# One-core attention and feed-forward kernel: local attention of batches 1 to 7 in 22 blocks of 26 tokens on 32x32 blocks, with the turning on VectorE

## The chip, the cores and the metric

The kernel runs on one core of a Trainium2 chip. The metric is the device time of one execution in microseconds (us), the median of the runs shown; less is better. The engines are named as in the profile: PE (TensorE, matmuls), PEld (its weight loads), DVE (VectorE), ACT (ScalarE), POOL (GpSimd) and SP (SyncE, which here only issues transfers).

## What is computed

Eight batches of eight heads, 576 tokens, head dimension 64. Each head gets two attentions: one over tokens pooled four to one (144 of them), whose output is repeated four times, and a local one in which a token sees the three neighbours on either side. Their sum, 4608 tokens by 512, goes through a two-layer feed-forward net.

```python
q_d, k_d, v_d = (a.reshape(B, H, 144, 4, D).mean(axis=3) for a in (q, k, v))
out_up = np.repeat(sm_attn(q_d, k_d, v_d), 4, axis=2)
mask = np.abs(pos[:, None] - pos[None, :]) < 4
scores = np.where(mask, scale * np.matmul(q, k.transpose(0, 1, 3, 2)), -1e9)
out_local = np.matmul(softmax(scores), v)
x = (out_up + out_local).transpose(0, 2, 1, 3).reshape(4608, 512)
h = x @ w_in
g = np.where(h >= 1, h, np.where(h <= -1, 0.0, (h + 1) ** 2 / 4))
return g @ w_out
```

(shortened: `scale` is 1/8, `softmax` subtracts the row's maximum)

## The kernel before

**Feed-forward.** The 4608 tokens are nine chunks of 512. Chunks 0 and 1 compute `x @ w_in` directly (L1045), chunks 2 to 8 by Strassen-Winograd products of 256x256 quarters (L1135); both feed `g @ w_out` (L1073). All are 128-row matmuls in three terms of split floats. Weights are loaded and split in chunk 0 (L852 to L873). DVE and ACT form `g` (L1011 to L1027) and the Winograd sums (L1141, L1144).

**Attention.** Heads go in pairs, 32 in all, numbered n; the two heads of a pair sit on partitions 0 to 63 and 64 to 127. Pairs 0 to 3 (batch 0) come first, as the start of the kernel, since chunk 0 needs all four. The 28 pairs of batches 1 to 7 are laid between the matmuls of chunks 0 to 6, four to a chunk; chunks 7 and 8 have none. For one of these 28 pairs:

- scores (L423, L468), one PE step: 20 matmuls of 64x64 for ten windows of 64 tokens in two heads, and six of 64x144 for the pooled scores, on 64x64 tiles of the array. A tile is given by where the operands lie (which head: 64 rows) and where the output goes (64 output partitions), so there are four. `QUARTERS` fixes the order of the steps. For g below 4 a window of head h goes to output half h; for g = 4 and for the pooled blocks it goes to the other half. So the two tiles "head h to half h" get eight window matmuls each, and the other two get two windows and three pooled blocks each.
- softmax of the windows, 128x640: band (L527), maximum (L530), subtraction on POOL (L532), exponential on ACT (L534), sum (L575), reciprocal (L579, L580), product (L583). The pooled softmax runs beside it (L558, L559, L565, L594, L595).
- transposes, one PE step with the 128x128 array: five for the windows (L652), three and one for the pooled part (L677, L678). ACT copies them out (L686, L701), DVE a masked piece (L705).
- values, one PE step on 64x64 tiles: 20 matmuls with 53 to 61 columns (L730) and eight for the pooled part (L753), then the joining on ACT and DVE (L808, L810, L821) into `xr`.

The trace counts two records for each float32 matmul that is not a transpose, so 20 matmuls show as x40.

**Order.** A planner (`Plan`) gives each step an engine, an assumed cost, keys and buffers, and places steps greedily; each engine then runs its steps in the order that this gives, fixed before the launch. The table `K` holds the keys. Loads all go through SP's queue, in order.

**Start.** PE runs ten warming matmuls on `ident` (L278), then the pairs of batch 0. Pair 0 has its values pooled by PE (L623, ten matmuls with the constant `fours`), and its pooled output is repeated four times inside PE (L773, 16 matmuls); the others have their values pooled on POOL (L604, L607). For pair 3 POOL also subtracts the maximum (L532).

Of the kernel before, what the change touches and what calls it, by code (L numbers as in the profile page):

```python
# [76 lines left out]
class Plan:  # L77
# [32 lines left out]
    def run(self):  # L110
# [7 lines left out]
        free = {"PE": 5.0, "ACT": 3.0, "DVE": 1.0, "POOL": 1.4, "SP": 0.7}  # L118
# [130 lines left out]
def attention_then_ffn(ctx: ExitStack, tc, qT, kT, vw, vp, vq, band, fours, w_in, w_out, out):  # L249
# [97 lines left out]

    def attention(n):
        b, p = pairs[n]
        early = n < K["early"]  # L350
        first = b == 0
        shares = b >= WIDE
        flat = shares or n < K["flat"]
# [23 lines left out]
        l_q = op("SP", 0.72 if b < 2 else 0.95, lambda: nc.sync.dma_start(qb.tile, qT[b, p]), bufs=[qb], key=k0 - ld, name=name + "lq")  # L377
        l_k = op("SP", 0.72 if b < 2 else 0.95, lambda: nc.sync.dma_start(kb_.tile, kT[b, p]), bufs=[kb_], key=k0 - ld, name=name + "lk")
# [3 lines left out]
        if not by_pe:  # L382
            vpb = sbuf("vp", [P if shares else KB, NKB, FACTOR, P], F32, "w" if 0 < n < 4 else "vp", range(8, 16) if 0 < n < 4 else [0])
            vsrc = vq[b - WIDE, p] if shares else vp[b, p]
            l_vp = op("SP", 1.7 if shares else 1.85, lambda: nc.sync.dma_start(vpb.tile, vsrc.rearrange("k (n f c) -> k n f c", n=NKB, f=FACTOR)),
                      bufs=[vpb], key=k0 - lv, name=name + "lvp")
        l_v = op("SP", 0.82 if b < 2 else 1.1, lambda: nc.sync.dma_start(vb.tile, vw[b, p].rearrange("k (n d) -> k n d", n=NB)),
# [14 lines left out]
        slp = psum([(0, 1, 2)] if shares else pairs_of_banks)  # L402
        spp = slp if shares else psum([(u,) for pair in pairs_of_banks for u in pair] if flat and first else [(2,)] if flat else pairs_of_banks)
# [46 lines left out]
        SPB = 2 if shares else 0  # L450
# [7 lines left out]
        def sp_view():  # L458
            return spp.tile[:, SPB, 0 : NSP * SD].rearrange("p (n s) -> p n s", n=NSP)
# [20 lines left out]
        if shares:  # L480

            def all_scores():
                if early:
                    add_band()
                for step in QUARTERS:
                    (window_scores if len(step) > 1 else pooled_block)(*step)

            o_sl = o_sp = op("PE", 1.46 if early else 1.10, all_scores, [l_q, l_k, o_qd, o_kd, before.get("x")], [slp, qb, kb_, qdb, kdb], kk[1], name=name + "sl", mode=1)
        else:
# [788 lines left out]
```

## Time and profile before

| what | value |
|---|---|
| time, median of 3 runs | 924.33 us (919.49 to 925.19) |
| the profiled execution's own time | 923.9 us |
| its span, first to last instruction | 921.8 us |
| PE, DVE, ACT, POOL busy in the span | 903.3, 654.2, 538.0, 125.8 us |
| mean granted TensorE clock | 0.996 |
| chain that ended last: PE, DVE, ACT, DMA | 89%, 4%, 3%, 3% |

PE is busy nearly all the time, so the time of the kernel is read as the sum of what PE issues, plus the start before chunk 0. Matmuls are pipelined: the length of a record is not its price. The price of a PE step is the distance from its first record to the first record of the step behind it.

### The profile page before, as it was taken

The numbers are of one execution on the slowest core, as the hardware profiler recorded it, in microseconds if no ns is written. First come the engines' busy times: TensorE is split into PE (matmuls) and PEld (weight loads), VectorE is DVE, ScalarE is ACT, GpSimd is POOL, SyncE is SP. The second block draws the span as 40 slices with busy tenths as digits, with TensorE's granted clock in tenths as the row PEclk, the third lists the DMA queues.
The fourth block names the chain that finished last, engine by engine and source line by source line (L and its number), as shares of the span: only waits on it lengthen the run. The fifth ranks groups of instructions, "written<-read, shape, count | busy, mean of one in ns | idle before, by whom it ended". The sixth has DMA issues, their size and how long they took to land.

```text
span 921.8 us, 20432 instructions
## 1 busy us (share of the span) xinstructions
PE 903.3 (98%) x8254; PEld 778.6 (84%) x8254; DVE 654.2 (71%) x1139; ACT 538.0 (58%) x1072; POOL 125.8 (14%) x126
## 2 busy tenths in 40 slices
PE   7799999999999999999999999999999999999998
PEld 6577788888888888888888888888888889989996
DVE  6799986888968775777867676877687755453543
ACT  4788896555565555556655555655555655444542
POOL 5222131111111110111111111111011000000000
PEclk9899999999999999999999999999999999999999
DMA  9997342664576656666576657665675456445631
GB/s 268 392 390 261 98 143 73 242 227 163 181 250 232 209 189 209 226 221 217 200 242 224 221 181 253 227 220 180 223 234 201 157 170 235 161 161 189 233 103 46
DMA packets 66170, 190.13 MB, mean 206 GB/s; under 512 B 7364, under 2 KB 9540, under 8 KB 66076
## 3 DMA queue, kind: packets, MB, share of 16 engines
q1 hardware_dynamic: 61468, 180.44, 57.2%
q10 hardware_dynamic: 4608, 8.39, 2.4%
q8 instruction: 65, 1.06, 0.5%
q14 instruction: 29, 0.24, 0.1%
HBM read 164.68 MB, written 24.12 MB: 205 GB/s over the span
## 4 chain that ended last, share of the span: by engine, by line
PE 89%; DVE 4%; ACT 3%; DMA 3%; issue 1%; SPq 0%; POOL 0%; ACTq 0%; DVEq 0%
PE ps L1073 41%; PE ps L1135 29%; PE ps L1045 9%; PE ps L730 2%; PE ps L423 2%; PE ps L652 2%; DMA vp<-vq 1%; PE ps L753 1%; PE ps L677 1%; PE ps L468 1%; DMA kf<-kT 1%; DVE gt L1027 1%; DVE tt L1144 1%; DMA out<-tt 1%; DVE tt L1023 1%
## 5 line engine op out<-in xcount | busy, mean ns | idle before, releaser
L1073 PE MATMUL ps<-w_o,gt 128*128 128x512 f32 x1728 | 439.8, 395 | 0.1
L1073 PEld LDWEIGHTS ps<-w_o,gt 128*128 128x128 f32 x1728 | 310.3, 188 | 58.0 <-DVE gt L1027 0.6
L1135 PE MATMUL ps<-T,lS 128*128 128x256 f32 x1008 | 147.9, 283 | 1.6 <-ACT tt L1141 1.6
L1135 PEld LDWEIGHTS ps<-T,lS 128*128 128x128 f32 x1008 | 133.9, 189 | 7.9 <-ACT tt L1141 3.9
L1011 ACT ACTIVATE tt<-tt 128x512 f32<-128x512 f32 x112 | 70.6, 630 | 108.1 <-DVE tt L1144 94.5
L1023 DVE SCALAR_TENSOR_TENSOR tt<-tt 128x512 f32<-128x512 f32 x112 | 83.7, 748 | 56.3 <-ACT tt L1016 54.7
L1025 ACT CAST gt<-tt 128x512 fp32r<-128x512 f32 x136 | 84.5, 621 | 62.8 <-DVE tt L1023 52.7
L1027 DVE TENSOR_TENSOR gt<-tt,gt 128x512 fp32r<-128x512 f32 x136 | 96.8, 712 | 32.8 <-ACT gt L1025 29.3
L1141 ACT COPY tt<-ps 128x512 f32<-128x512 f32 x112 | 65.3, 585 | 83.5 <-PE ps L1135 80.6
L1135 PE MATMUL ps<-B,lA 128*128 128x256 f32 x672 | 101.3, 286 | 0.3 <-DVE tt L1144 0.2
L1135 PEld LDWEIGHTS ps<-B,lA 128*128 128x128 f32 x672 | 90.6, 189 | 12.9 <-DVE tt L1144 5.8
L1045 PE MATMUL ps<-x,w_i 128*128 128x512 f32 x384 | 95.2, 397 | 1.0 <-ACT x L897 0.4
L1016 ACT ACTIVATE tt<-tt 128x512 f32<-128x512 f32 x144 | 91.0, 632 | 4.4
L1045 PEld LDWEIGHTS ps<-x,w_i 128*128 128x128 f32 x384 | 71.1, 188 | 18.9 <-ACT x L897 0.8
L1144 DVE TENSOR_TENSOR tt<-tt 128x512 f32<-128x512 f32 x56 | 41.8, 746 | 58.9 <-ACT tt L1141 58.7
L1144 DVE TENSOR_TENSOR tt<-ps,tt 128x512 f32<-128x512 f32 (+1 forms) x112 | 62.1, 554 | 28.8 <-PE ps L1135 27.7
L607 POOL TENSOR_TENSOR vd<-vp 128x256 f32<-128x256 f32 (+1 forms) x31 | 23.3, 750 | 347.4 <-PE ps L753 336.0
L604 POOL TENSOR_TENSOR vp<-vp 128x512 f32<-128x512 f32 (+1 forms) x31 | 43.4, 1399 | 130.8 <-DMA vp<-vq 127.7
L532 POOL TENSOR_TENSOR sl<-sl,mxl 128x640 f32<-128x640 f32 x29 | 40.4, 1392 | 89.6 <-DVE mxl L530 89.4
L1135 PEld LDWEIGHTS ps<-B,lS 128*128 128x128 f32 x336 | 45.6, 188 | 6.6 <-DVE tt L1144 2.5
L1135 PE MATMUL ps<-B,lS 128*128 128x256 f32 x336 | 50.9, 287 | 0.1
L1135 PE MATMUL ps<-T,lA 128*128 128x256 f32 x336 | 48.8, 281 | 0.0
(111 smaller groups left out, 1058.9 us busy)
## 6 DMA issues: line engine op xcount, KB each, us to landing
lS<-S SPq DMA_DIRECT2D x112, 512.0 KB, 4.4
lA<-A SPq DMA_DIRECT2D x56, 512.0 KB, 3.7
vp<-vq SPq DMA_DIRECT2D x28, 512.0 KB, 4.8
lA<-A SPq DMA_DIRECT2D x56, 256.0 KB, 3.2
v<-vw SPq DMA_DIRECT2D x32, 320.0 KB, 3.6
raw_i<-w_in SPq DMA_DIRECT2D x16, 512.0 KB, 8.9
raw_o<-w_out SPq DMA_DIRECT2D x16, 512.0 KB, 8.2
out<-tt ACTq DMA_DIRECT2D x32, 256.0 KB, 2.2
```

The source lines that it names most:

```text
L532: o_s = op("POOL", 1.3, lambda: nc.gpsimd.tensor_tensor(slf(), slf(), ml_n(), op=ALU.subtract), [o_m], [slb, mlb], kk[2], name=name + "sub ...
L604: nc.gpsimd.tensor_tensor(vpb.tile[:, :, 0:2, :], vpb.tile[:, :, 0:2, :], vpb.tile[:, :, 2:4, :], op=ALU.add)
L1011: o2 = op("ACT", 0.49 + e, lambda: nc.scalar.activation(u(), src(), AF.Relu, bias=0.5, scale=0.5), deps, [srcbuf, ub], key, name=f"relu {n ...
L1016: nc.scalar.activation(u(), u(), AF.Square)
L1023: o4 = op("DVE", v, lambda: nc.vector.scalar_tensor_tensor(g(), src(), 1.0, u(), op0=ALU.max, op1=ALU.min), [o3], [srcbuf, ub], key, name= ...
L1025: o5 = op("ACT", 0.50 + e, lambda: nc.scalar.copy(flat(gb.tile[:, 0]), g()), [o4], [held, gb], key, name=f"gh {name}")
L1027: engine.tensor_tensor(flat(gb.tile[:, 1]), g(), flat(gb.tile[:, 0]), op=ALU.subtract)
L1045: nc.tensor.matmul(hb.tile[:, 0, :], wb.tile[:, w, cc * P : (cc + 1) * P], xt[:, x], start=cc == 0 and i == 0, stop=cc == NCC - 1 and i == 2)
L1073: nc.tensor.matmul(o, gb.tile[:, g, ts], wb.tile[:, w, :], start=i0 + i == 0, stop=i0 + i == 3 * NFC - 1)
L1135: nc.tensor.matmul(xy(dst), l(w, k), yb.tile[:, v, k], start=first and n == 0, stop=n == 5, skip_group_check=True)
L1141: return op("ACT", cost, lambda: nc.scalar.copy(to(), src()), deps, [tb, XY], kk[i], name=f"{name} {c},{j}")
L1144: return op("DVE", cost, lambda: nc.vector.tensor_tensor(to(), a(), b(), op=ALU.add), deps, held, kk[i], name=f"{name} {c},{j}", port=port)
```

## The change

Pairs of batches 1 to 7 go through a new function, `banded`; pairs 0 to 3 keep the old one, without its branch for later batches (`shares`).

- The windows become 22 blocks to a head, each of 26 tokens (the last of each half fewer or more) with 32 queries and 32 keys. A score block is a 32x32 output, so the scores use tiles of 64 rows and 32 columns, eight of them (two heads, four quarters of the output partitions). There are 40 matmuls of 32x32, four of 32x64 (a 23rd place filled by a copy) and ten of 32x144. The table `ORDER` gives their order.
- The window softmax is 128x384 in place of 128x640.
- The product with the reciprocal (`norm`) writes each block twice, masked by `odd`, 128x768 into the tile of q and k; `nc.vector.transpose` then turns 32x32 blocks into `sl`. This takes the place of the five window transposes on PE and of ACT's copy of them. The q and k of the next pair can only be loaded behind it, since the tile is shared.
- The pooled part is turned by PE in five transposes, arranged so that one ACT copy of 128x448 serves; the masked DVE piece goes.
- Values: 24 matmuls (20 of 52 or 54 columns, four of 26 or 29) and the same eight for the pooled part.
- Pair 0 is still pooled by PE, but no longer repeated there: `pu1` goes from 4 to 0, so four matmuls of 64x144 stand where 16 of 192 or 96 columns stood, and ACT and DVE join the parts as for the other pairs.
- Constants: `band` and its 32-wide form come in one transfer on ACT's queue, not SP's; `ident` is now the copy `ident_r`, which ACT makes behind the two band copies, and the warming matmuls wait for it.
- The keys in `K` and some assumed costs are other numbers, so the order of many steps moves. POOL gets 15 of the weight splits (8 before) and DVE 17 (24 before).

```diff
+SW = 32
+SQ = SW - 2 * (FACTOR - 1)
+NS = 11
+SHORT = [[0] + [SQ + 1 + SQ * i for i in range(NS - 1)], [SQ * NS + 1 + SQ * i for i in range(NS)]]
+ORDER = ("P00 w13 w11 w02 w10 w12 w11 P13 w10 w03 w12 w10 w02 w01 P11 w00 P10 w01 w00 P12 w03 P02 w13 w03 w00 w01 w13 "
...
-    ident = cpool.tile([P, P], F32, name="ident")
-    make_identity(nc, ident)
-    band_sb = cpool.tile([P, WIN], F32, name="band_sb")
-    nc.sync.dma_start(band_sb, band)
+    made = spool.tile([P, P + WIN + SW], F32, name="made", tag="w35")
+    nc.scalar.dma_start(made[:, P:], band)
+    make_identity(nc, made[:, 0:P])
     ident_r = cpool.tile([P, P], F32R, name="ident_r")
-    nc.scalar.copy(ident_r, ident)
+    nc.scalar.copy(ident_r, made[:, 0:P])
+    ident = ident_r.bitcast(F32)
...
+    def banded(n):
...
+        def scores():
+            seen = {}
+            for kind, h, c in ((x[0], int(x[1]), int(x[2])) for x in ORDER):
+                hs = slice(h * D, (h + 1) * D)
+                n = seen[kind, h, c] = seen.get((kind, h, c), -1) + 1
+                if kind == "w":
+                    w, cols, lhs, rhs = start_of(c // 2, 2 * n + c % 2), slice(n * SW, (n + 1) * SW), q_(), k_()
+                    bank, rhs = h, rhs[hs, w : w + SW]
...
+                else:
+                    w, cols, lhs, rhs = (SD - SW) * h if n else TAIL * (1 - h) + SW * c, slice(LC, LC + SD), qdb.tile, kdb.tile[hs, :]
+                    bank = 2 if n else h
+                nc.tensor.matmul(slp.tile[c * SW : (c + 1) * SW, bank, cols], lhs[hs, w : w + SW], rhs, start=True, stop=True)
...
+        o_a = op("DVE", 0.56, lambda: nc.vector.tensor_tensor(slv(), local(), bands, op=ALU.add), [o_sl], [slp, slb], kk[2], name=name + "band")
+        o_m = op("DVE", 0.55, lambda: nc.vector.tensor_reduce(mlw(), slw(), axis=AX.X, op=ALU.max), [o_a], [slb, mlb], kk[2], name=name + "max")
...
+        def recip():
+            nc.vector.tensor_scalar_add(sums(), sums(), 1e-9)
+            nc.vector.reciprocal(sums(), sums())
+            nc.vector.tensor_tensor(scaled(), sums()[:, 0:NW].unsqueeze(2).broadcast_to([P, NW, 2]), odd.unsqueeze(1).broadcast_to([P, NW, 2]), op=ALU.mult)
...
+        o_n = op("DVE", 0.96, lambda: nc.vector.tensor_tensor(
+            sn().rearrange("p (w a k) -> p w a k", a=2, k=SW), slw().unsqueeze(2).broadcast_to([P, NW, 2, SW]),
+            scaled().unsqueeze(3).broadcast_to([P, NW, 2, SW]), op=ALU.mult), [o_r], [slb, qk, slp], kk[4], name=name + "norm")
+        o_t = op("DVE", 0.98, lambda: nc.vector.transpose(slb.tile, sn()), [o_n], [slb, qk], kk[4], name=name + "turn")
...
+        def turns():
+            t = turned()
+            turn(apart(t, 0, M0), spb.tile[:, 2, 0:P], ident)
+            turn(apart(t, M0, P + 2 * TAIL), tailb.tile[:, 5 * TAIL : 5 * TAIL + P], ident)
+            for h in range(2):
+                turn(t[:, TAIL + h * P : TAIL + (h + 1) * P], spb.tile[:, h, 0:P], ident)
+            turn(t[:, M0 + TAIL : M0 + TAIL + P], tailb.tile[:, 0:P], ident)
...
+        def values():
+            for g in range(NG2):
+                for x, h in ((0, 0), (1, 1), (1, 0), (0, 1)):
...
+                    nc.tensor.matmul(pl_s()[hs, o[2 * g] : o[2 * g] + two * n], vb.tile[rs, h, g, :], m, start=True, stop=True)
...
     def attention(n):
         b, p = pairs[n]
+        if b >= WIDE:
+            return banded(n)
...
-    pv1=1, pu1=4, o1=-7.22, o2=32.66, dk0=-1.45, tl=12.56, ts=3.47, sd=-82.32, sw=68.59, sl=13.82, nq=0.45, dk1=-3.13,
+    pv1=1, pu1=0, o1=3.56, o2=32.66, dk0=-0.05, tl=-13.06, ts=0.62, sd=-76.44, sw=55.44, sl=14.22, nq=0.41, dk1=-4.42,
```

In the orders below a name such as `qk_355` is a tile and its number; numbers differ between the kernels.

On PE, the scores of pair 4, the first of batch 1, in chunk 0. Before:

```order
L423 MATMUL ps<-k_277,q_268 64x64 x8
L468 MATMUL ps<-kd_534,qd_84 64x144 x2
L423 MATMUL ps<-k_277,q_268 64x64 x4
L468 MATMUL ps<-kd_534,qd_84 64x144 x2
L423 MATMUL ps<-k_277,q_268 64x64 x4
L468 MATMUL ps<-kd_534,qd_84 64x144 x2
L423 MATMUL ps<-k_277,q_268 64x64 x4
```

And now, the first 12 of 26 rows of the same step:

```order
L429 MATMUL ps<-kd_473,qd_85 32x144
L429 MATMUL ps<-qk_355 32x32 x6
L429 MATMUL ps<-kd_473,qd_85 32x144
L429 MATMUL ps<-qk_355 32x32 x6
L429 MATMUL ps<-kd_473,qd_85 32x144
L429 MATMUL ps<-qk_355 32x32
L429 MATMUL ps<-kd_473,qd_85 32x144
L429 MATMUL ps<-qk_355 32x32 x2
L429 MATMUL ps<-kd_473,qd_85 32x144
L429 MATMUL ps<-qk_355 32x32
L429 MATMUL ps<-kd_473,qd_85 32x144
L429 MATMUL ps<-qk_355 32x32 x5
```

The 26 matmuls of the step became 54, smaller ones, with the pooled blocks spread among them.

On DVE, the second half of a pair's window softmax in the Winograd chunks, between steps of the feed-forward (L1144, L1023 and L1027 before; L1304, L1183 and L1187 now). Before:

```order
L575 TENSOR_REDUCE ps<-sl_4300 128x10
L579 TENSOR_SCALAR ps<-ps 128x13
L580 RECIPROCAL ps<-ps 128x13
L1023 SCALAR_TENSOR_TENSOR tt<-tt 128x2x256
L1144 TENSOR_TENSOR tt<-ps,tt 128x256
L583 TENSOR_TENSOR sl_4300<-sl_4300,ps 128x640
L1027 TENSOR_TENSOR gt<-tt,gt 128x512
L1023 SCALAR_TENSOR_TENSOR tt<-tt 128x512
L594 TENSOR_TENSOR sp_4330<-sp_4330,ps 128x128
L595 TENSOR_TENSOR sp_4330<-sp_4330,ps 128x3x112
```

And now, for a pair in the same stretch:

```order
L487 TENSOR_SCALAR ps<-ps 128x15
L488 RECIPROCAL ps<-ps 128x15
L489 TENSOR_TENSOR ps<-ps,odd 128x24
L1304 TENSOR_TENSOR tt<-tt 128x2x256
L492 TENSOR_TENSOR qk_4520<-sl_4691,ps 128x768
L1304 TENSOR_TENSOR tt<-ps,tt 128x2x256
L495 STREAM_TRANSPOSE sl_4691<-qk_4520 128x768
L506 TENSOR_TENSOR spt<-sp_4743,ps 128x2x3x16
L507 TENSOR_TENSOR sp_4743<-sp_4743,ps 128x3x128
L1183 SCALAR_TENSOR_TENSOR tt<-tt 128x2x256
```

Two operations of 768 elements, the product and the turn, stand where one of 640 stood, and the feed-forward's steps are woven between them.

On POOL, in the start: the pooling of values (vp, vd) and the subtraction for pair 3 (sl). Before:

```order
L604 TENSOR_TENSOR vp_186<-vp_186 72x2x256
L607 TENSOR_TENSOR vd_304<-vp_186 72x256
L604 TENSOR_TENSOR vp_193<-vp_193 72x2x256
L607 TENSOR_TENSOR vd_364<-vp_193 72x256
L604 TENSOR_TENSOR vp_297<-vp_297 128x2x256
L532 TENSOR_TENSOR sl_395<-sl_395,mxl_407 128x640
L604 TENSOR_TENSOR vp_308<-vp_308 72x2x256
L607 TENSOR_TENSOR vd_455<-vp_308 72x256
```

And now:

```order
L827 TENSOR_TENSOR vp_192<-vp_192 72x2x256
L828 TENSOR_TENSOR vd_315<-vp_192 72x256
L827 TENSOR_TENSOR vp_248<-vp_248 72x2x256
L828 TENSOR_TENSOR vd_374<-vp_248 72x256
L827 TENSOR_TENSOR vp_293<-vp_293 72x2x256
L828 TENSOR_TENSOR vd_436<-vp_293 72x256
L767 TENSOR_TENSOR sl_332<-sl_332,mxl_397 128x640
L514 TENSOR_TENSOR vp_371<-vp_371 128x2x256
```

The subtraction stood behind the values of pair 4 (`vp_297`, 128 partitions); now it stands ahead of them and behind those of pair 3.

## Rows read from the trace of the kernel before

**Rows 1.** The page: busy time of engines, and the chain that ended last.
```profile
PE 903.3 (98%) x8254; PEld 778.6 (84%) x8254; DVE 654.2 (71%) x1139; ACT 538.0 (58%) x1072; POOL 125.8 (14%) x126
PE 89%; DVE 4%; ACT 3%; DMA 3%; issue 1%; SPq 0%; POOL 0%; ACTq 0%; DVEq 0%
```
**Rows 2.** Windows: stretch, length, busy PE PEld DVE ACT POOL, clock, DMA share, GB/s.
```profile
0.00:40.00 40.00, 29.51 (x514) 24.64 (x514) 26.39 (x47) 22.18 (x55) 17.12 (x35) 0.91 0.97 324
442.60:541.80 99.20, 99.15 (x996) 86.95 (x996) 72.80 (x133) 57.05 (x116) 14.35 (x12) 1.00 0.64 218
752.50:836.60 84.10, 83.51 (x523) 75.02 (x522) 37.97 (x60) 40.36 (x69) 0.00 (x0) 1.00 0.54 185
```
**Rows 3.** Timeline of PE, scores of one pair: start, length, what, records.
```profile
445.71 0.88 PE L1135 MATMUL ps<-T,lS 128*128 128x256 f32 x6
446.52 0.46 PE L423 MATMUL ps<-k,q 64*64 64x64 f32 x16
446.80 0.29 PE L468 MATMUL ps<-kd,qd 64*64 64x144 f32 x2
...
447.05 0.29 PE L468 MATMUL ps<-kd,qd 64*64 64x144 f32 x2
...
447.22 0.28 PE L423 MATMUL ps<-k,q 64*64 64x64 f32 x4
447.29 0.29 PE L468 MATMUL ps<-kd,qd 64*64 64x144 f32 x2
447.34 0.28 PE L423 MATMUL ps<-k,q 64*64 64x64 f32 x4
...
447.63 0.98 PE L1135 MATMUL ps<-B,lA 128*128 128x256 f32 x6
```
**Rows 4.** Timeline of PE, transposes and values of the same pair.
```profile
458.30 0.86 PE L1073 MATMUL ps<-w_o,gt 128*128 128x512 f32 x3
459.00 0.71 PE L652 MATMUL ps<-ident,sl 128*128 128x128 f32 x5
459.55 0.49 PE L677 MATMUL ps<-ident,sp 128*112 128x128 f32 x3
459.88 0.27 PE L678 MATMUL ps<-ident,sp 128*128 128x128 f32 x1
459.90 1.64 PE L1073 MATMUL ps<-w_o,gt 128*128 128x512 f32 x6
...
465.68 0.80 PE L730 MATMUL ps<-al,v 64*64 64x61 f32 x40
466.30 0.56 PE L753 MATMUL ps<-ap,vd 64*64 64x144 f32 x16
466.79 0.98 PE L1135 MATMUL ps<-B,lS 128*128 128x256 f32 x6
```
**Rows 5.** Groups by line and shape, DVE and ACT: count, busy us, mean ns, idle.
```profile
L527 DVE TENSOR_TENSOR sl<-ps,band_sb 128x640 f32<-128x640 f32 x29 | 23.8, 822 | 13.4 <-PE ps L423 12.4 <-PE ps L468 0.6
L821 DVE TENSOR_TENSOR xr<-ps,xd 128x256 f32<-128x256 f32 x4 | 1.7, 414 | 0.0
L705 DVE TENSOR_TENSOR ap<-ps,odd 128x192 f32<-128x192 f32 x28 | 9.9, 354 | 7.6 <-PE ps L678 7.6
L686 ACT COPY al<-ps 128x640 f32<-128x640 f32 x32 | 22.1, 689 | 13.9 <-PE ps L677 9.6 <-PE ps L652 2.1 <-ACT tt L1084 2.0
```
**Rows 6.** Timelines of the start, by engine; in brackets idle time ahead and releaser.
```profile
1.45 4.64 PE L278 MATMUL ps<-ident 128*128 128x128 f32 x20 [1.45 <-POOL ident masks.py:199]
40.07 1.66 PE L1045 MATMUL ps<-x,w_i 128*128 128x512 f32 x6
```
**Rows 7.** The same of ACT, POOL and DVE.
```profile
2.67 0.29 ACT L260 CAST ident_r<-ident 128x128 fp32r<-128x128 f32 x1
23.43 1.27 POOL L604 TENSOR_TENSOR vp<-vp 128x512 f32<-128x512 f32 x1 [2.53 <-DMA vp<-vq]
26.72 0.83 DVE L575 TENSOR_REDUCE ps<-sl 128x10 f32<-128x640 f32 x1 [1.85 <-ACT sl L534]
```

More of the change, by code (lines that the diff above doesn't have):

```diff
@@ L117, in run @@
         engines = ["PE", "ACT", "DVE", "POOL", "SP"]
-        free = {"PE": 5.0, "ACT": 3.0, "DVE": 1.0, "POOL": 1.4, "SP": 0.7}
+        free = {"PE": 5.0, "ACT": 3.0, "DVE": 1.0, "POOL": 1.4, "SP": 0.75}
         ready = {e: [] for e in engines}
@@ L401, in attention @@
         pairs_of_banks = [(0, 1), (2, 3), (4, 5), (6, 7)] if first else [(0, 1)]
-        slp = psum([(0, 1, 2)] if shares else pairs_of_banks)
-        spp = slp if shares else psum([(u,) for pair in pairs_of_banks for u in pair] if flat and first else [(2,)] if flat else pairs_of_banks)
+        slp = psum(pairs_of_banks)
+        spp = psum([(u,) for pair in pairs_of_banks for u in pair] if flat and first else [(2,)] if flat else pairs_of_banks)
         hab = sbuf("half", [P, 2 * SD], F32, "w", SLOTS) if first else temp(2) if b == 1 else None
@@ L478, in pooled @@
                 pooled_block(i)
[L480 to L489, printed above, removed]
-            o_sl = op("PE", 1.46 if flat else 1.23, scores, [l_q, l_k, None if extra else before.get("tl" if first else "x")], [slp, qb, kb_], kk[1], name=name + "sl", mode=1)
-            o_sp = op("PE", 0.90 if flat else 0.64, pooled, [o_qd, o_kd, None if extra else before.get("tp")], [spp, qdb, kdb], kk[2], name=name + "sp", mode=1, after=(o_sl, 0.12) if flat else None)
+        o_sl = op("PE", 1.46 if flat else 1.23, scores, [l_q, l_k, None if extra else before.get("tl" if first else "x")], [slp, qb, kb_], kk[1], name=name + "sl", mode=1)
+        o_sp = op("PE", 0.90 if flat else 0.64, pooled, [o_qd, o_kd, None if extra else before.get("tp")], [spp, qdb, kdb], kk[2], name=name + "sp", mode=1, after=(o_sl, 0.12) if flat else None)
         mlb = sbuf("mxl", [P, NB], F32, "mxl", [0, 1])
@@ L502, in ml_n @@
             return mlb.tile.unsqueeze(2).broadcast_to([P, NB, WIN])
-        less = early and n in PE_MAX(K)
         if early:
@@ L807, in attention @@
         xdb = scratch("xd", [P, SD], "xd")
-        o_xd = op("ACT", 0.29, lambda: nc.scalar.mul(xdb.tile, pp_v(not shares), 1.0 if by_pe else 1.0 / FACTOR), [o_pp], [plp, xdb], kk[9], name=name + "xd")
-        if shares:
-            o_xd = op("DVE", 0.30, lambda: nc.vector.scalar_tensor_tensor(xdb.tile, pp_v(1), 1.0 / FACTOR, xdb.tile, op0=ALU.mult, op1=ALU.add),
-                      [o_xd], [plp, xdb], kk[9], name=name + "xe")
+        o_xd = op("ACT", 0.29, lambda: nc.scalar.mul(xdb.tile, pp_v(), 1.0 if by_pe else 1.0 / FACTOR), [o_pp], [plp, xdb], kk[9], name=name + "xd")
         if extra:
```

344 lines of the change are left out of this document (225 added, 119 removed).

## Prediction, made before the changed kernel had run

> **What bounds the kernel now.** I read the page first: PE is busy for 903.3 of 921.8 us, and the chain that ended last is 89% PE [rows 1]. Then the busy times by stage. In the start, up to 40 us, PE is busy for 29.51 and DVE for 26.39, while the DMA engines are busy 0.97 of the time; there the kernel waits. In a Winograd chunk with four attention pairs PE is busy for 99.15 of 99.20 us at clock 1.00, DVE for 72.80, ACT for 57.05, POOL for 14.35. The chunk without pairs takes 84.10 [rows 2]. So from 40 us on the time is the sum of what PE issues, and four pairs cost 99.20 - 84.10 = 15.1 us, 3.8 us each. A change to attention is worth what it takes from those 3.8 us, times 28 pairs, plus what it does to the start. Third, the timeline of one pair shows the three PE steps: scores from 446.52 to 447.63, 1.11 us [rows 3]; transposes from 459.00 to 459.90, 0.90; values from 465.68 to 466.79, 1.11 [rows 4]. These make 3.12; the rest of the 3.8 is the slow first matmuls behind each step and some waits, which I take as unchanged, since there are still three steps.
>
> **Transposes.** Nine become five of the same 128x128 kind. The first five start 0.55 us ahead of the sixth, 0.11 each, and the next three take 0.33, again 0.11 [rows 4]. Four fewer: -0.44 us a pair. This term is the surest.
>
> **Scores.** Two paces first. Between 447.22 and 447.34 four window records start on two tiles, two each, so a record with 64 columns holds its tile for 0.06 us. The pooled records come at 446.80, 447.05 and 447.29, two to a tile in each 0.245, so one with 144 columns holds it for 0.123 [rows 3]. Before, the tiles with eight window matmuls (16 records) are full for 0.96, the other two (six pooled records, four of windows) for 0.74 + 0.24 = 0.98, and 0.13 of the 1.11 is entry and exit. Now the fullest of the eight tiles, by the table of the order, gets six blocks (12 records with 32 columns) and two pooled ones (4 records). No row shows a record of 32 columns on a 64x32 tile, so I bound it. Half of 0.06 is the floor: 12 x 0.03 + 4 x 0.123 = 0.85, -0.13. The full 0.06 is the ceiling: 0.72 + 0.49 = 1.21, +0.23. A line through 0.06 at 64 and 0.123 at 144 columns gives 0.035 at 32 and 0.91 in all, -0.07. As eight queues in one program order will not be packed as well as four, I take 0.
>
> **Values.** 40 records on four tiles, ten each, take from 465.68 to 466.30, 0.062 a record [rows 4]. There are now 12 on each tile, with the same 1152 columns in all. By records that is +0.12, by columns 0; I take the middle, +0.06.
>
> PE per pair: -0.44 + 0 + 0.06 = -0.38, times 28: **-10.6 us**. The bounds are -0.44 - 0.13 = -0.57 (-16.0 us) and -0.44 + 0.23 + 0.12 = -0.09 (-2.5 us).
>
> **DVE, ACT, POOL in the chunks.** On DVE 640 elements take 822 ns and 256 take 414 [rows 5]: 1.06 ns an element and 0.14 us an operation. Gone are four operations of 640 (3.28) and the masked piece of 0.354. New are three of 384 (0.55 each, 1.65), the product with 768 (0.96), a small product of 24 (0.17) and the turn of 768. The turn has no row. At the pace of an elementwise operation it takes 0.96, at half that pace 1.77, and as little as half of 0.96 if it were a faster copy. I take 0.96, since it reads and writes as many elements as the product. Together 3.74 against 3.63: DVE does 0.1 us more a pair, on an engine that is idle 26 of 99 us, so PE covers it. If that cover were gone it would cost 3 us in the kernel, or 26 with the slow turn. ACT loses the copy of 689 ns [rows 5] and has more room. The subtraction on POOL shrinks with 640 to 384, and POOL is 14% busy. The loads of the next q and k now wait for the turn. Pairs are 24.8 us apart (99.20 over four), the transposes of before start 12.5 us behind the scores [rows 3, 4] with the window product ahead of them, and the DMA engines are 0.64 busy, so this stays hidden; but SP's queue is in order, and a late turn would hold the products' operands that stand behind those loads.
> The new thing is the block of work in DVE's queue: product, turn and the small product take 2.09 us where 0.82 stood, and the feed-forward's sums that release PE stand behind them. I allow +1.0 us for the kernel.
>
> **Start.** Two additions. The warming matmuls began at 1.45 [rows 6]; they now need the copy of the identity, which was made from 2.67 to 2.96 [rows 7] and has one more small copy ahead of it, so about 3.1: +1.7 us. DVE gets the joining of pair 0 and two sums that POOL made, three operations of 576 elements at 0.75: +2.25. Two waits go: POOL sat for 2.53 us on the values of pair 4 with pair 3's subtraction behind it, and DVE sat 1.85 behind that [rows 7]; the subtraction now stands ahead of them. The PE repetition of pair 0 goes too, but PE is not full here. All added and nothing gained is +4.0; all waits gone and nothing exposed is -4.4. The waits lie on the chain, the additions on engines that are idle a third of the time, so I take -1.0. The first projection then starts near 39 where it started at 40.07 [rows 6].
>
> **Sum.** Made against the profiled execution's own time, 923.9 us (span 921.8), which is 0.4 below the median of 924.33: 923.9 - 10.6 + 1.0 - 1.0 = **913.3 us**.
>
> **Rivals.**
> A. A block of 32 columns is no cheaper than one of 64. Each record holds its tile for 0.06, the scores grow by 0.23, a pair gains only 0.15, and the kernel 4.2: 919.7 us. For it: windows of 53 to 61 columns ran at 0.062, no faster than 64 at 0.06 [rows 3, 4]. Against it: 144 columns take only twice as long as 64, so the pace does follow columns above that. [...]
> B. The slower side: eight tiles are fed from one instruction stream, and records cannot start fast enough. In the scores 16 records start between 446.52 and 446.80, 17.5 ns each [rows 3]. If that is the limit of the stream rather than of the tiles, 108 records take 1.89 + 0.13 = 2.02 us, +0.91 a pair, +25.5: 938.8 us. It decides the sign from a scores step of 1.11 + 0.38 = 1.49 us on. Against it: in the values 40 records over four tiles fit their tiles' pace, so the tiles are the limit there. [...]
> C. DVE's block starves PE: of the 1.27 us that it has grown by, half reaches PE at each pair, 0.64 x 28 = 18: 931 us. Against it: the block of before left 0.05 us of idle PE in a whole chunk [rows 2].
> D. More than forecast: scores at -0.13, values at 0 and the start at -4.4: 923.9 - 16.0 + 1.0 - 4.4 = 904.5 us.
>
> **How the numbers follow.** Forecast (908 to 918) 0.60; A 0.15; B 0.07; C 0.07; D 0.11. The range reaches down to D and up past A, into C: 904 to 926. It leaves out B, most of C and what lies below D, about 0.15. About 1%, 9.2 us, is what a measurement of this kernel can tell from no change, so faster begins below about 915. The forecast lies mostly below (0.40 of its 0.60), and D wholly: faster 0.51. The rest of the forecast, A and half of C are within 1%: 0.39. B and the other half of C: slower 0.10.
>
> **What the profile will show.** If I am right, in a pair of the Winograd chunks: scores from first record to the next product in 1.0 to 1.2 us, five transposes in about 0.46, values in 1.11 to 1.23, the turn near 0.96, a chunk with four pairs in 97 to 98 us, and the first projection near 39. A shows as scores of 1.3; B as scores above 1.49; C as PE waits on DVE sums (L1304) or on `gt` that were 0.05 us a chunk; a wrong start as a first projection outside 36 to 44. The forecast is wrong if the scores are outside 0.98 to 1.34, or if chunks with pairs shrink by less than 0.5 us while the steps shrink as said.

## The result, and the profile after

The changed kernel takes 929.16 us (median of 13 runs, 926.64 to 935.02), the kernel before 922.71 in the same comparison (13 runs, 919.49 to 925.19). The ratio is 1.0069, 95% interval 1.0054 to 1.0084: 0.7% slower, less than the 1% that the prediction set as its bound, and outside its range of 904 to 926. The profiled execution took 929.51 us, with a span of 927.7 against 921.8 before.

The page of the changed kernel: busy time of the engines, the queue `q8 instruction` (packets, MB, share of the DMA engines), and the chain that ended last. [rows 1] are the same of before.

```profile
PE 900.6 (97%) x9910; PEld 776.9 (84%) x9910; DVE 658.5 (71%) x1163; ACT 517.3 (56%) x1044; POOL 125.9 (14%) x130
q8 instruction: 78, 1.28, 0.6%
PE 83%; DVE 7%; ACT 4%; DMA 3%; issue 2%; ACTq 0%; POOL 0%; DVEq 0%; POOLq 0%
```

PE still sets the time. It issues 9910 matmul records in place of 8254 and yet is busy for 2.7 us less; the chain has lost 6 points of PE, and DVE (+3), ACT (+1) and "issue" (+1) have gained. In the kernel before this queue moved 65 packets:

```profile
q8 instruction: 65, 1.06, 0.5%
```

Timeline of PE, the scores of one pair in a Winograd chunk (start, length, what, records), as [rows 3] of before:

```profile
454.76 0.85 PE L1295 MATMUL ps<-B,lS 128*128 128x256 f32 x6
455.54 0.31 PE L429 MATMUL ps<-kd,qd 64*32 64x144 f32 x1
455.55 0.27 PE L429 MATMUL ps<-qk 64*32 64x32 f32 x11
...
455.88 0.40 PE L429 MATMUL ps<-kd,qd 64*32 64x144 f32 x2
456.01 0.23 PE L429 MATMUL ps<-qk 64*32 64x32 f32 x2
...
456.73 0.33 PE L429 MATMUL ps<-qk 64*32 64x32 f32 x13
456.99 0.97 PE L1233 MATMUL ps<-w_o,gt 128*128 128x512 f32 x3
```

From the first record to the next product 1.45 us, where it was 1.11. Transposes and values of the same kind of pair, as [rows 4]:

```profile
471.69 1.54 PE L1233 MATMUL ps<-w_o,gt 128*128 128x512 f32 x6
473.07 0.27 PE L529 MATMUL ps<-ident_r,sp 128*128 128x128 f32 x1
...
473.50 0.27 PE L529 MATMUL ps<-ident_r,spt 128*128 128x128 f32 x1
473.53 0.96 PE L1295 MATMUL ps<-B,lA 128*128 128x256 f32 x6
...
475.13 0.90 PE L572 MATMUL ps<-sl,v 64*64 64x54 f32 x48
475.85 0.46 PE L582 MATMUL ps<-ap,vd 64*64 64x144 f32 x8
476.12 0.30 PE L579 MATMUL ps<-ap,vd 64*64 64x72 f32 x8
476.36 0.97 PE L1295 MATMUL ps<-T,lS 128*128 128x256 f32 x6
```

Transposes 473.07 to 473.53, 0.46 us where it was 0.90; values 475.13 to 476.36, 1.23 where it was 1.11.

For all 28 pairs I took each step's price from the records of both traces: from the start of the last product ahead of it to the start of the first one behind it, less what that product takes among its own kind. It includes entry and exit, so it is 0.09 to 0.1 above the lengths just read for scores and values. Medians in us:

| step of a pair | before | after | change | predicted | x 28 |
|---|---|---|---|---|---|
| scores (52, then 108 records) | 1.208 | 1.538 | +0.33 | 0 | +9.2 |
| transposes (9, then 5) | 0.901 | 0.464 | -0.437 | -0.44 | -12.2 |
| values (56, then 64) | 1.204 | 1.325 | +0.12 | +0.06 | +3.4 |

What the transposes save, the scores and values take back: +0.4 us in the kernel by medians, and +2.2 by the sums over all pairs, since single steps hold a longer gap. The rest of the 5.9 us between the spans is the start, with the first projection at 43.58 in place of 40.07 (+3.5), and the gaps of over 30 ns between products outside the steps (17.8 us in all before, 19.1 after, +1.3). The shorter gaps between the 4464 product records, which are read to 1 ns, come out 1.1 us less.

The waits of PE from 45 us on (for what; us in total, times, longest), before:

```profile
PE ps L1135 <- ACT tt L1141: 1.6, 3, 0.6
PE ps L730 <- ACT al L686: 1.1, 1, 1.1
PE ps L1045 <- DVE tt L1023: 0.3, 1, 0.3
PE ps L1135 <- DVE tt L1144: 0.2, 1, 0.2
```

and after:

```profile
PE ps L1295 <- DVE tt L1304: 1.6, 4, 0.4
PE ps L1295 <- issue: 1.4, 1, 1.4
PE ps L1295 <- ACT tt L1301: 1.0, 1, 1.0
PE ps L1295 <- DVE T L1102: 0.8, 4, 0.2
PE ps L429 <- issue: 0.7, 1, 0.7
```

Two things are new. Four times, once in each of the Winograd chunks 3 to 6, PE waits 0.4 us for DVE's sums (L1304) and 0.2 for `T`: 2.4 us in all, where before it waited 0.2 for DVE's sums. And twice it waits for nothing that the profile shows ("issue"), 2.1 us; more on this below.

The start, rows of PE and ACT of the changed kernel (in brackets the idle time ahead and what ended it), as [rows 6, 7]:

```profile
4.28 4.12 PE L294 MATMUL ps<-ident_r 128*128 128x128 f32 x20 [4.28 <-ACT ident_r L273]
8.63 0.99 PE L686 MATMUL ps<-kf,qf 64*64 64x64 f32 x34
33.14 1.47 PE L877 MATMUL ps<-ident_r,sp 128*72 128x128 f32 x6 [6.57 <-DVE sp L820]
43.58 1.65 PE L1205 MATMUL ps<-x,w_i 128*128 128x512 f32 x6 [1.67 <-DVE xr L981]
```

```profile
3.67 0.24 ACT L276 CAST band_r<-made 128x64 fp32r<-128x64 f32 x1 [1.23 <-DMA made<-band]
3.94 0.29 ACT L273 CAST ident_r<-made 128x128 fp32r<-128x128 f32 x1
```

On ACT the copy of the identity stands behind the two copies of the band, and the first of these waits for the constant's transfer. So the warm-up starts 2.8 us later and the first scores at 8.63, where they stood at 6.53.

### The profile page after: what moved, and what is told of

It reads as the page before. It is cut to its first block, busy times and chain, and to the rows that moved or that the text cites. A ratio compares the mean times of both kernels' runs of the same rounds, so it can differ in the third digit from the quotient of the medians.

```text
span 927.7 us, 23785 instructions
## 1 busy us (share of the span) xinstructions
PE 900.6 (97%) x9910; PEld 776.9 (84%) x9910; DVE 658.5 (71%) x1163; ACT 517.3 (56%) x1044; POOL 125.9 (14%) x130
## 4 chain that ended last, share of the span: by engine, by line
PE 83%; DVE 7%; ACT 4%; DMA 3%; issue 2%; ACTq 0%; POOL 0%; DVEq 0%; POOLq 0%
PE ps L1233 36%; PE ps L1295 27%; PE ps L1205 9%; PE ps L429 5%; PE ps L572 2%; DMA qk<-qT 2%; PE ps L529 1%; DVE tt L1183 1%; ACT tt L1171 1%; PE ps L582 1%; DVE gt L1187 1%; ACT sp L480 1%; DVE tt L1304 1%; DMA out<-tt 1%; ACT tt L1176 1%
## 5 line engine op out<-in xcount | busy, mean ns | idle before, releaser
L1187 DVE TENSOR_TENSOR gt<-tt,gt 128x512 fp32r<-128x512 f32 x137 | 99.1, 724 | 22.8 <-ACT gt L1185 21.5
L1183 DVE SCALAR_TENSOR_TENSOR tt<-tt 128x512 f32<-128x512 f32 x112 | 79.5, 710 | 50.5 <-ACT tt L1176 49.6
L1304 DVE TENSOR_TENSOR tt<-ps,tt 128x512 f32<-128x512 f32 x112 | 62.1, 554 | 41.3 <-PE ps L1295 41.1
L517 POOL TENSOR_TENSOR vd<-vp 128x256 f32<-128x256 f32 x28 | 24.6, 877 | 332.4 <-PE ps L579 308.5
L1304 DVE TENSOR_TENSOR tt<-tt 128x512 f32<-128x512 f32 x56 | 39.0, 696 | 43.2 <-ACT tt L1301 43.2
L480 ACT ACTIVATE sp<-ps,mxp 128x144 f32<-128x144 f32 x84 | 32.0, 381 | 39.3 <-DVE mxp L474 33.1
L514 POOL TENSOR_TENSOR vp<-vp 128x512 f32<-128x512 f32 x28 | 39.5, 1411 | 87.3 <-DMA vp<-vq 87.3
```

Source lines behind the costliest of these rows:

```text
L480: nc.scalar.activation(spb.tile[:, i], sp_view()[:, i], AF.Exp, bias=mxb.tile[:, i : i + 1], scale=scale, accum_out=sums()[:, NW + i : NW ...
L1183: o4 = op("DVE", v, lambda: nc.vector.scalar_tensor_tensor(g(), src(), 1.0, u(), op0=ALU.max, op1=ALU.min), [o3], [srcbuf, ub], key, name= ...
L1187: engine.tensor_tensor(flat(gb.tile[:, 1]), g(), flat(gb.tile[:, 0]), op=ALU.subtract)
L1304: return op("DVE", cost, lambda: nc.vector.tensor_tensor(to(), a(), b(), op=ALU.add), deps, held, kk[i], name=f"{name} {c},{j}", port=port)
```

## The experiments

My theory after reading the result: the scores grew because something other than the tiles' own work limits them. The rivals are the order (a matmul whose tile is busy holds up those behind it) and the feeding of many small matmuls. Apart from these stands the start. All numbers are compared with the kernel before on the same chip; each ratio has its 95% interval.

**The warm-up's identity.**

```diff
-        nc.tensor.matmul(ps[:, 7, 0:P], ident, ident, start=True, stop=True)
+        nc.tensor.matmul(ps[:, 7, 0:P], made[:, 0:P], made[:, 0:P], start=True, stop=True)
```

> The changed kernel, with the ten warm-up matmuls reading the identity where GpSimd writes it (made) instead of the rounded copy that ScalarE makes at 3.94 us; all else the same. Theory 'the warm-up is the late start': in the changed kernel the first warm-up matmul starts at 4.28 us and the first scores at 8.63, before at 1.45 and 6.53, so the scores move up by 2.1 to 2.8, VectorE's first score reduction from 10.41 to about 8, the first projection from 43.58 to about 41.3, and the whole from 929.2 to about 927. Rival 'VectorE sets the start anyway': the pooled sums of the first banded pair and the normalisations on VectorE fill what is gained, first projection 43 or later, 928.5 to 929.5.

926.62 us, ratio 1.0022 (1.0006 to 1.0038) where the changed kernel has 1.0069. PE's timeline of the start:

```profile
1.56 4.64 PE L294 MATMUL ps<-made 128*128 128x128 f32 x20 [1.56 <-POOL made masks.py:199]
6.45 0.99 PE L686 MATMUL ps<-kf,qf 64*64 64x64 f32 x34
41.68 3.66 PE L1205 MATMUL ps<-x,w_i 128*128 128x512 f32 x13 [1.66 <-DVE xr L981]
```

The scores start 2.2 us earlier and the first projection 1.9. The other runs bear this out: in the nine profiles with the late warm-up (the changed kernel's among them) the first projection starts at 43.6 to 46.9, in the four with the early one at 40.5 to 42.2. The theory holds for these 1.9 of the 3.5 us; about 1.6 us of the start remain in this trace.

**The order of the score matmuls.** First two sorted orders, all pooled matmuls behind the blocks or ahead of them:

```diff
-ORDER = ("P00 w13 w11 w02 w10 w12 w11 P13 w10 w03 w12 w10 w02 w01 P11 w00 P10 w01 w00 P12 w03 P02 w13 w03 w00 w01 w13 "
-         "P03 w00 w13 P01 w11 w00 w13 w10 w02 w11 w00 P13 w02 P00 w12 w03 w02 w10 w12 w01 w02 w11 w12 w01 w03 w12 w10").split()
+def _order():
+    tiles = [(0, 0), (1, 2), (0, 1), (1, 3), (0, 2), (1, 0), (0, 3), (1, 1)]
+    blocks = [f"w{h}{c}" for n in range(NG2) for h, c in tiles if 2 * n + c % 2 < NS]
+    return blocks + [f"P{h}{c}" for h, c in tiles] + ["P00", "P13"]
+
+ORDER = _order()
```

> The changed kernel, with the 54 score matmuls of a banded pair in another order: the 44 block matmuls first, going round the eight tiles, then the pooled ones, one a tile, then the two second ones. Same instructions, same tiles, same banks. Theory 'order': in the changed kernel a block matmul whose tile is busy with a pooled one (two records of 0.123 us) holds up all that stand behind it; with the pooled ones last nothing is held up, and the step falls from 1.54 us to the work of the fullest tile, 12 x 0.032 + 4 x 0.123 = 0.88, and its entry and exit, 1.0 to 1.2 in all: 28 x 0.35 to 0.5 = 10 to 15 us, so 914 to 919. Rival 'stream': 108 records cost 0.0142 us each whatever their order, step 1.54, 929. Rival 'banks': the four tiles of one half write one PSUM bank at a time; in this order the pairs of banks are as evenly used as before, so no change, 929.

926.12 us, ratio 1.0033 (1.0014 to 1.0051), step 1.477. With the list of the eight pooled ones ahead of `blocks` in the return, and the two second ones still at the end:

> As the run with the pooled matmuls last, but with the eight first pooled matmuls ahead of the 44 block matmuls, and the two second ones at the end. Theory 'order': every block matmul of the first round waits for its tile's pooled one, but all tiles are free at about the same time, so the step is again about that of the fullest tile, 1.0 to 1.25 us, 914 to 920. Rival 'stream': 1.54 us, 929. [...]

927.93 us, ratio 1.0047 (1.0022 to 1.0073), step 1.516. Neither theory: the order is worth 0.02 to 0.06 us a pair, not 0.35 to 0.5, but it is worth something. The timeline of one pair with the pooled ones last:

```profile
452.99 0.85 PE L1300 MATMUL ps<-B,lS 128*128 128x256 f32 x6
453.78 0.94 PE L434 MATMUL ps<-qk 64*32 64x32 f32 x86
454.52 0.29 PE L434 MATMUL ps<-kd,qd 64*32 64x144 f32 x1
...
454.54 0.69 PE L434 MATMUL ps<-kd,qd 64*32 64x144 f32 x18
455.16 0.73 PE L1238 MATMUL ps<-w_o,gt 128*128 128x512 f32 x2
```

Sorted like this the records are easily told apart, and their starts show how the step is fed. In ns from the first:

```
records 1 to 32    0 7 13 20 27 33 40 46 52 59 66 72 79 84 86 ... 149 156 162     6.6 apart at first, 162 in all
then               240 271
then               280 296 313 331 346 363 380 396 413 430 446 ...                a new matmul every 16.6
```

Every matmul makes two records. The first 16 matmuls start within 0.16 us, nothing new starts for about 0.12 us, and from then on a new matmul starts every 16.6 ns. The 37 that are left then take 0.61 us, although all tiles are free (a tile's turn comes every eighth matmul, 0.13 us, and its two records take 0.06): 0.280 + 0.614 = 0.894, and the two second pooled ones, which wait for their tile, end it at 1.169. In this trace 34 matmul records and 34 weight loads start ahead of the even pace. Why these start so much closer together than the later ones isn't shown.

**Twice as many blocks.** The same order, each block matmul issued twice:

```diff
+                for _ in range(2 if kind == "w" else 1):
                     nc.tensor.matmul(slp.tile[c * SW : (c + 1) * SW, bank, cols], lhs[hs, w : w + SW], rhs, start=True, stop=True)
```

> The order with the pooled matmuls last, with each of the 44 block matmuls issued twice in a row into the same place (the same result is written twice): 88 more records in a pair. Theory 'order' (the fullest tile sets the step): 12 more records of 0.032 us on it, the step 0.38 us longer than with the pooled ones last, 28 x 0.38 = 11 us above that run. Rival 'stream': 88 more records at 0.0142 us, 1.25 us a pair, 35 us above that run.

1040.05 us, ratio 1.126 (1.118 to 1.135). In the shortest steps 44 more matmuls cost 1.0 us (2.47 in place of 1.477), 22.6 ns each: well over the 0.38 of the fullest tile, and also over the 0.73 that they would cost at 16.6 ns. But the median step is 5.1 us, and steps of up to 8.9 us were not expected by either. PE's rows where this happens, and its first line among the waits:

```profile
415.23 0.30 PE L435 MATMUL ps<-kd,qd 64*32 64x144 f32 x2
419.85 0.77 PE L435 MATMUL ps<-kd,qd 64*32 64x144 f32 x15 [4.32 <-issue]
```

```profile
PE ps L435 <- issue: 53.6, 18, 5.1
```

```profile
q8 instruction: 97, 1.59, 0.6%
```

PE stands in the middle of a step without a semaphore to wait for. In each of the 18 gaps of over 1.5 us in score steps a packet of the instruction queue lands, and PE goes on 1.2 to 1.6 us after it; here the packet moved from 417.6 to 418.5. There are 97 packets in place of 78, of 16.4 KB each (1.59 MB over 97). That PE lacked instructions is inferred from these times; no run took the packets away.

**Fewer matmuls, the same columns.**

```diff
-                    if 2 * n + c % 2 == NS - 2:
+                    if n % 2:
+                        continue
+                    if n % 2 == 0:
                         cols, rhs = slice(n * SW, (n + 2) * SW), rhs.unsqueeze(1).broadcast_to([D, 2, SW])
```

> The order with the pooled matmuls last, and of the 44 block matmuls of a pair only every second one of a tile is issued, over 64 columns in place of 32 (its scores stand a second time in its neighbour's place, so the attention of every second block is left out): the same columns, 34 matmuls in place of 54. Theory 'feed' (each matmul after the first 16 costs 16.6 ns): 20 fewer are 0.33 us, so first to last record 0.80 to 0.85 in place of 1.17, step about 1.13, 10 us below the run with the pooled ones last (926.1), 916. Rival 'columns on a tile': the columns are the same, 1.48 and 926.

920.71 us, ratio 0.9971 (0.9949 to 0.9994), step 1.195. One pair:

```profile
450.00 0.85 PE L1302 MATMUL ps<-B,lS 128*128 128x256 f32 x6
450.79 0.67 PE L436 MATMUL ps<-qk 64*32 64x64 f32 x44
...
451.30 0.65 PE L436 MATMUL ps<-kd,qd 64*32 64x144 f32 x16
451.89 0.50 PE L1240 MATMUL ps<-w_o,gt 128*128 128x512 f32 x1
```

From the first record to the next product 1.10 us, with the pooled ones last 1.38. Twenty matmuls fewer over the same columns save 0.28 us, 14 ns each (0.33 was expected): the number of matmuls is what costs, and the rival of the columns falls. New matmuls start 16.6 ns apart here too, though each has 64 columns. At 34 matmuls the step is as long as before the change. What sets the pace isn't separated: the weight loads, two to a matmul, became fewer with the matmuls.

**Orders from this model.** If the feed is all, an order in which no tile is busy when its turn comes should take 0.95 us from first to last record. I laid one out:

```diff
+ORDER = ("w13 P10 w11 w03 w02 w01 w00 w12 P13 w11 w02 P00 w12 w01 w03 P02 w01 w10 w12 w13 w11 w03 w00 P12 w01 w13 w10 "
+         "w00 w03 w11 P13 w10 w02 w03 w00 w11 P01 w02 w00 w12 w10 P03 w02 w00 w12 w13 w10 P11 P00 w02 w13 w01 w12 w10").split()
```

> The changed kernel, with its 54 score matmuls of a banded pair in a third order, laid out from what the traces of the first orders show: the first 16 matmuls of the step start within 0.16 to 0.46 us (the quicker, the less a busy tile holds them up), about 0.12 us pass, and from there on a new matmul starts every 16.6 ns (37 of them, 0.61 us); in this order no matmul should find its tile busy when its turn comes. Theory 'feed': first to last record 0.94 to 1.0 us, the step 1.18 to 1.25 us, 0.29 to 0.36 below the changed kernel's 1.54, 28 x that = 8 to 10 us, so 919 to 921. Rival 'stream with a fixed price for a record': 1.48 to 1.54 as in the other orders, 926 to 929.

932.6 us, ratio 1.0097 (1.0060 to 1.0135): not faster than the changed kernel, and the two intervals overlap. With the early warm-up as well:

> The same, with the warm-up matmuls reading the identity where GpSimd writes it as well (that edit alone took the first projection from 43.58 to 41.68 us). If the two add up: 8 to 10 us and 1.9 to 2.5 off 929.2, so 916.5 to 919.5, under the kernel before (923.3). If the feed theory falls: 924 to 927.

929.54 us, ratio 1.0060 (1.0031 to 1.0089). The layout fails: the step is 1.60. Three more orders asked what in it does the harm. Two pooled matmuls among the last blocks of other tiles:

```diff
+ORDER = ("w00 w12 w01 w13 w02 w10 w03 w11 w00 w12 w01 w13 w02 w10 w03 w11 w00 w13 w12 w01 w00 w13 w02 w10 w00 w13 w03 "
+         "w11 w00 w12 w01 P00 P13 w02 w10 w03 w11 w12 w01 w02 w10 w03 w11 w12 w02 w10 P12 P01 P00 P13 P02 P10 P03 P11").split()
```

> The changed kernel, with the score matmuls in a fourth order: block matmuls round the tiles, the two tiles that have a second pooled matmul done with their blocks first and their first pooled one at places 31 and 32 of 54, the other blocks, then the other pooled ones with the two second ones among them. So only two pooled matmuls have blocks of other tiles behind them, and no matmul's own tile is busy when its turn comes. With all pooled ones last the step was 1.477 (its end waits 0.27 us for the two second ones). Theory 'own tile': without a wait for the own tile there is no hole; first to last record about 1.03, step 1.33, 4 us below the order with the pooled ones last, 922. Theory 'mixed sizes': a pooled matmul that runs beside blocks of other tiles makes a hole of about 0.1 us, as in the paced order (1.602) and the changed kernel's (1.538): step 1.43 or more, 925 to 928.

926.17 us, ratio 1.0022 (1.0003 to 1.0040). Pooled ones first in one half of the rows, blocks first in the other:

```diff
+ORDER = ("P00 w10 P01 w11 P02 w12 P03 w13 w10 w11 w12 w13 w10 w11 w12 w13 w00 w10 w01 w11 w02 w12 w03 w13 w00 w10 w01 "
+         "w11 w02 w12 w03 w13 w00 w10 w01 w12 P13 w02 P10 w03 P11 w00 P12 w01 w02 w03 w00 w01 w02 w03 w00 w02 P13 P00").split()
```

> The changed kernel, with the score matmuls in a fifth order: in one half of the array's rows (head 0) the pooled matmuls come first and the blocks after them, in the other half (head 1) the blocks first and the pooled ones in the middle; the two second ones at the end. Sizes are mixed between the halves, hardly within one. Theory 'mixed sizes, anywhere': holes of about 0.1 us as in the changed kernel, step 1.5 or more, 928. Theory 'mixed sizes within a half': no hole, first to last record about 1.05, step 1.35, 923 to 924. Theory 'own tile': no hole either, 1.35, 923 to 924; the run with two pooled ones early tells these two apart.

931.18 us, ratio 1.0073 (1.0049 to 1.0098). And the two pooled ones at places 15 and 16, with the early warm-up:

```diff
+ORDER = ("w00 w12 w01 w13 w02 w10 w03 w11 w00 w13 w12 w01 w02 w10 P00 P13 w03 w11 w12 w01 w02 w10 w03 w11 w00 w12 w01 "
+         "w13 w02 w10 w03 w11 w00 w12 w01 w13 w02 w10 w03 w11 w00 w12 w13 w02 w10 w00 P00 P13 P12 P01 P02 P10 P03 P11").split()
```

> Warm-up on GpSimd's identity, and the score matmuls in a sixth order: block matmuls round the tiles, but the two tiles with a second pooled matmul get their first one at places 15 and 16, so that it runs in the 0.12 us in which no matmul starts after the first 16; all other pooled ones last. It differs from the pooled-last order with the same start (923.75, step 1.478) in this alone. Theory 'own tile and feed': no hole, the end no longer waits 0.27 us for the second ones, first to last record 1.03, step 1.34, 28 x 0.14 = 3.9 us less, 920, under the kernel before (923.9). Theory 'mixed sizes': blocks of other tiles stand behind the two pooled ones, a hole of about 0.1 us as with two early, step 1.44 to 1.53, 923 to 925.

924.17 us, ratio 1.0010 (0.9989 to 1.0031). All orders, by the records of one undisturbed pair (us):

| order | until the even pace begins | first to last record | step |
|---|---|---|---|
| pooled last | 0.280 | 1.169 | 1.477 |
| two early | 0.281 | 1.218 | 1.525 |
| two at places 15, 16 | 0.330 | 1.153 | 1.460 |
| changed kernel | 0.464 | 1.302 | 1.538 |
| pooled first | 0.465 | 1.208 | 1.516 |
| one half of the rows each | 0.465 | 1.417 | 1.724 |
| paced | 0.488 | 1.295 | 1.602 |

Where several pooled matmuls stand among the first 16, it takes 0.46 to 0.49 until the even pace begins, 0.18 more than with blocks alone. Later the stream stops once more in some orders. In the changed kernel and in the paced one this is in the middle of the step, for 0.100 and 0.092 us, at about the 36th and the 40th matmul; with two at places 15 and 16 for 0.052, at about the 31st. With two early it isn't behind those two: the blocks there run on, with gaps of at most 0.03. The gap of 0.109 us stands where only pooled ones are left, and the next matmul to start is the second one of `P00` (pooled, head 0, quarter 0). It comes 0.131 us behind the last start, at 0.990, although its tile's last record before it began at 0.675. With the rows it is the same: the second of `P13` starts behind the blocks without a gap, and the second of `P00`, the last of all, 0.131 behind it. The end of the step is then only the second records of the last matmuls, 144 ns behind the first ones.

So "own tile" alone doesn't explain these gaps, and "mixed sizes" as it was set out isn't shown either, for in the two orders made to tell them apart the gap has no block behind it. What holds the stream up there stays open.

The ratios don't follow the steps closely. By its step the order with two early should gain 0.4 us on the changed kernel, and by the ratios it gains 4.3; the rows should lose 5.2 and lose 0.4. The runs are from several chips and the intervals are 1.4 to 3.5 us to either side, so what a step costs is read from the traces.

**Pooled last and early warm-up together.** Both edits from above.

> The order with the pooled matmuls last (926.1) and the warm-up on GpSimd's identity (2.5 us off) together: 923.0 to 924.5 if they add up, the same as the kernel before (923.6); over 925 if the time saved at the start is lost again on the way.

923.75 us, ratio 0.9998 (0.9974 to 1.0022), first projection at 40.45. They add up, and within the interval the result equals the kernel before. No version here is measurably faster than the kernel before and computes the same.

**The values' records.**

```diff
-                        m = bass.AP(tensor=m.tensor, offset=m.offset, ap=[m.ap[0], [c0[1] - c0[0], 2], [1, n]])
+                        m = bass.AP(tensor=m.tensor, offset=m.offset, ap=[m.ap[0], [1, 2 * n]])
```

> The changed kernel, with each block-pair matmul of the values step reading one run of 52 neighbouring columns in place of two runs of 26 (so the columns are shifted and the local part of the output isn't the reference's): same records, same columns. In the changed kernel such a record follows the last on its tile after 58.5 ns. Theory 'two runs cost': a run of 52 takes about 53 ns by the 58 ns that 58 columns took before, 12 x 5.5 ns = 0.07 us off the step of 1.325. Rival 'a record's fixed price': 58.5 ns stay, 1.325.

928.79 us in one run, step 1.326: unchanged. The two runs of 26 columns aren't what costs. In the changed kernel the records of a tile follow each other after 58.4 ns with 52 columns, before after 58.3 with 58; two records more on each tile are then 0.117 us, which is the step's growth. The number of columns isn't what sets it: in the same step the second record of a matmul with 26 or 29 columns is also followed by the next matmul after 58 to 59 ns (its first record by the second after 36 to 37). Why the tile is held so long stays open.

## Why the prediction was wrong

**The bound** was right: PE is busy 97% and what it issues sets the time from the first projection on.

**Transposes**: right, -0.437 against -0.44.

**Scores**: this is the term that failed. The sum counted the work of the fullest tile, and weighed the rest in one sentence: "As eight queues in one program order will not be packed as well as four, I take 0". The tile's own price was right: on one tile, records of 32 columns follow each other after 31 to 33 ns, close to the 0.035 of the line through the two known paces. So rival A, with its 0.06 for 32 columns, is refuted. But the tile's 0.85 to 0.91 us is not the only bound. The feed is another: with the pooled ones last, 0.28 us and 37 times 16.6 ns, 0.89, pass before the two second pooled ones, although no tile is busy. In the changed kernel's order the pooled ones among the first 16 add 0.18 and the gap in the middle 0.10; about 0.13 of the 1.302 from first to last record are spread over smaller gaps. Of the step's growth by 0.33 the experiments account for 0.28 by the number of matmuls (54 in place of 34) and 0.06 by the order. This is rival B's mechanism. B had its price as 17.5 ns for each record and all or nothing, which would have made 2.02 us; it is 16.6 ns for each matmul of two records, and only behind the first 16. The step came to 1.45 from first record to next product, above the ceiling of 1.34 and below B's 1.49. At the head of the step records start 6.6 ns apart on different tiles. B was right to ask for the rate, and the row that it used, 16 records in 0.28 us, was one in which the tiles were the limit: the trace of before has them start in fours, 6.6 ns apart, with 58 ns from a tile's second record to its third and on.

**Values**: +0.12, the upper bound by records, where I took the middle. Of the 40 records of before all had 53 to 61 columns; no row showed how a record with fewer columns is priced on such a tile, and with 52 it is no cheaper (58.4 ns against 58.3 with 58).

**DVE in the chunks**: the turn takes 0.975 us against 0.96, the product of 768 elements 0.950 against 0.96. The groups of DVE after (count, busy us, mean ns):

```profile
L495 DVE STREAM_TRANSPOSE sl<-qk 128x768 f32<-128x768 f32 x28 | 27.3, 975 | 0.5
L492 DVE TENSOR_TENSOR qk<-sl,ps 128x768 f32<-128x768 f32 x28 | 26.6, 950 | 0.4
```

Rival C's sign showed, at a small size: the waits for DVE's sums and for `T` are 2.4 us in the kernel, against 1.0 allowed, and all gaps of over 30 ns between products together grew by 1.3.

**Start**: the sign was wrong, +3.5 in place of -1.0. The step that failed is "one more small copy ahead of it, so about 3.1": the copy ahead waited for the constant's transfer, until 3.67, and ACT made the identity's copy only behind it, at 3.94, though POOL had written the identity by 1.51. By the first experiment that is 1.9 of the 3.5 us. In the kernel before the copy of the band had started at 2.52, and PE's longest wait of the start was 3.78 (rows of ACT and of PE):

```profile
2.52 0.24 ACT L262 CAST band_r<-band_sb 128x64 fp32r<-128x64 f32 x1 [0.50 <-DMA band_sb<-band]
30.59 1.50 PE L663 MATMUL ps<-ident,sp 128*72 128x128 f32 x6 [3.78 <-DVE sp L597]
```

The waits that were to go came back elsewhere: DVE's 1.85 us [rows 7] went, and PE then stood 6.57 us for DVE's `sp`. The prediction laid the additions on engines that are idle a third of the time; but in the changed kernel DVE stands idle only 0.38 and 0.76 us between 10.41 and that `sp` at 32.39, and added sums of 0.74 to 0.75 us (L400, L981) stand ahead of it. The rest of the lateness probably comes from there; no run took these sums away. The good end of the term, -4.4, also added POOL's 2.53 and DVE's 1.85, though the second stood behind the first.

**Instructions**: not in the prediction at all. In the changed kernel's profile three gaps end 1.3 to 1.4 us behind an instruction packet (0.94 us at 302, 1.56 at 702, 1.15 at 854, 3.6 together); before there is none of this kind. They come and go: the profile with the early warm-up, with the same instructions, has none, those of the rows and of places 15 and 16 have one of 2.6 and 3.1 us. In this profile they are more than half of the 5.9 us between the spans, two of them within the gaps between products above and one in a score step. That execution, with 929.51, stands near the median of its kernel (929.16); how much of this is in the others isn't known.

**The range** stopped at 926, since B was priced only as a whole (938.8) and the start's bad end (+4.0) was not put together with any other case. A scores step between 1.34 and 1.49 with a late start is what came, and no case stood for it.

## What to carry to other kernels

When a step is cut into more and smaller matmuls on smaller tiles, count the matmuls, not only the columns of the fullest tile: here each one behind the first 16 to 17 cost 16.6 ns, so by this pace 54 take 0.9 us, and no order tried was shorter. Of the sorted orders the one with the short ones first was the shorter, 1.477 against 1.516 us a step, but sorting was worth 0.06 at most. And when a constant's path changes, look up what stands ahead of its copy in that engine's queue and what that waits for.

## What the runs showed of the hardware

- The second record of a matmul may start behind the first records of later matmuls: with the pooled ones first, eight records of 144 columns start 6.6 ns apart on eight tiles, and their second ones follow 147 ns behind them.
- After the first 16 to 17 matmuls of a step (34 records and 34 weight loads with the pooled ones last) no new one starts for about 0.12 us; then one every 16.6 ns, in all these orders.
- PE can stand in the middle of a step of many short matmuls without a semaphore to wait for: with the blocks twice the 28 score steps add up to 133 us, where 28 of the shortest would make 69. Each of the 18 long gaps ends 1.2 to 1.6 us behind an instruction packet; that it lacked instructions is inferred from this, no run shows it.
- On 64x32 tiles records of 32 columns follow each other after 31 to 33 ns; on 64x64 tiles those of 52 and of 58 columns both after 58, and behind the second record of a matmul it is 58 to 59 ns even with 26 columns.
